# Attention with a threshold: the thresholds of two steps come from one VectorE instruction

## The chip, the cores and the metric

The kernel runs on one core of one Trainium2 chip. The metric is the device time of an execution in microseconds, and the median of the runs stands for a kernel. TensorE is called PE, VectorE DVE, ScalarE ACT, GpSimd POOL and SyncE SP, as the profile does. PE has a separate stream for loading weights, PEld.

## The reference

Three layers follow each other. Only the first is touched here:

```
q, k, v: (4, 8, 576, 64)      tau = 0.02
scores = q @ k^T / sqrt(64)
thresh = max(scores, last axis) - tau
scores = where(scores >= thresh, scores, -1e9)
attn   = exp(scores - max(scores)); attn = attn / (sum(attn) + 1e-9)
x      = attn @ v
```

A rational mixture layer (2304 tokens, 512 to 2048 to 512) and a mixture of eight experts come after it.

## The kernel before

The attention is written as one loop of steps. A step `i` handles 128 query rows, and there are 144 of them: 16 units, each one head of two batches, 1152 rows in nine tiles `t` (0 to 8). Two units share a pair of K and Q tiles, so the pattern of work repeats every eighteen steps. The scores are kept with their sign turned, so the largest score is a minimum.

Every engine runs its own instructions in the order in which the loop emits them. Nothing is reordered, and the framework adds the semaphore waits. An instruction that reads what an earlier instruction of the same engine wrote also waits for that one's semaphore. The loop body of step `i` does this, in this order:

- `emit_s(i + 1)` (L383): PE computes the next step's scores into the PSUM tile `s`. There are three such tiles, so the scores of step `i` need the tile that step `i - 3` has finished with. In every third step this comes after `emit_pv` instead of before it.
- `emit_pv(i - 12)` (L445, L446): PE multiplies the probabilities, transposed, with V. It reads the tile `pt`, twelve steps late.
- `emit_e(i)`: DVE takes the row minimum into `mn[:, 0:1]` (L399, "the reduce"), and ACT takes the exponential into the tile `e`, with that minimum as its bias (L401, "Exp").
- `emit_thr(i)` in some steps, on ACT: `mn[:, 1:2] = mn[:, 0:1] + tau` (L408).
- `emit_p(i - 1)`: DVE compares the scores with the threshold and multiplies by `e` (L415, "the select"). ACT copies that to half precision (L420, "the copy"), and POOL computes what the copy lost (L421, "the remainder"). When `i - 1` is odd, SP then starts a transposing DMA from `php` to `pt` (L424) for that step and the one before it together. `php` is a ring of four such pairs.
- In every third step, `emit_x(..., 0)`: DVE takes the reciprocal of the row sums (L458).
- `emit_thr(i)` in the other steps, on DVE (L410).
- In every third step, `emit_x(..., 1)`: DVE multiplies by the reciprocals (L460).
- Then come steps of a plan written out by hand: PE transposes of Q and K (L242, L247), their copies on ACT (L258 to L269), sums and splits of V (L308, L342, L354, L355), loads, and the DMAs that rotate V.

Which engine makes the threshold is written in a string that repeats every nine steps, `s` for ACT and `v` for DVE:

```
THR = 'svvvsvvvv'
def emit_thr(i):
    mn = st[i][1]
    e = THR[i % len(THR)]
    if e == "s":
        nc.scalar.activation(mn[:, 1:2], mn[:, 0:1], AF.Identity, bias=tauc[:, 1:2])
    else:
        (nc.gpsimd if e == "g" else nc.vector).tensor_scalar(
            mn[:, 1:2], mn[:, 0:1], tauc[:, 1:2], 0.0, op0=ALU.add, op1=ALU.add)
```

So 32 of the 144 thresholds are made by ACT and 112 by DVE. The tile `mn` holds one step's minimum and threshold and has three buffers.

Later in the kernel, the second layer keeps per-column constants in a tile `cvs`. DVE writes two columns of each of its halves at a time (L816 to L821), and ACT reads single columns of it as scales and biases (L939, L940).

Of the kernel before, what the change touches and what calls it, by code (L numbers as in the profile page):

```python
# [9 lines left out]
F32 = mybir.dt.float32  # L10
# [4 lines left out]
AF = mybir.ActivationFunctionType  # L15
ALU = mybir.AluOpType
AX = mybir.AxisListType
PSUM = bass.MemoryType.PSUM
P = 128
# [134 lines left out]
    "xt6": -1,  # L154
}
X_LAG = 0
THR = 'svvvsvvvv'
SUM_ACT = (1, 3)
SUM_AT = (0, 1, 1, 2, 3)
LO_POOL = ()  # L160
# [3 lines left out]
def attention(nc, tc, q, k, v, tau, xT, vs, ident, tail):  # L164
# [7 lines left out]
    def pool(c, name, bufs, **kw):  # L172
        return c.enter_context(tc.tile_pool(name=name, bufs=bufs, side="right", reuse_waits="tile", **kw))

    fix = pool(ctx, "fix", 1)
    sm = pool(ctx, "sm", 3)
# [11 lines left out]
    N = NU * UT  # L188
# [12 lines left out]
    tauc = fix.tile([P, 3], F32, name="tauc")  # L201
# [170 lines left out]
    st = {}  # L372

    def emit_s(i):
        u, t = divmod(i, UT)
        g, hh = divmod(u, 2)
        kt = KT[g].rearrange("p t c -> p (t c)")
        ps = ps_s.tile([P, 2, 512], F32, tag="s", name="s")

        def qk(po, m, qt, bb):  # L380
            for half in range(2):
                c = (2 * bb + half) * 288
                nc.tensor.matmul(  # L383
                    ps[po:po + m, half, 0:288], qz[:, g % 2, hh, t, qt:qt + m],
                    kt[:, c:c + 288], start=True, stop=True)

        if t < 4:
            qk(0, P, 0, 0)
        elif t == 4:
            qk(0, 64, 0, 0)  # L390
            qk(64, 64, 64, 1)
        else:
            qk(0, P, 0, 1)
        st[i] = ps

    def emit_e(i):
        ps = st[i]
        mn = sm.tile([P, 2], F32, tag="mn", name="mn")
        nc.vector.tensor_reduce(mn[:, 0:1], ps[:, :, 0:288], axis=AX.XY, op=ALU.min)  # L399
        e = e_p.tile([P, 2, 288], F32, tag="e", name="e")  # L400
        nc.scalar.activation(e, ps[:, :, 0:288], AF.Exp, bias=mn[:, 0:1], scale=-1.0)  # L401
        st[i] = (ps, mn, e)

    def emit_thr(i):
        mn = st[i][1]
        e = THR[i % len(THR)]
        if e == "s":
            nc.scalar.activation(mn[:, 1:2], mn[:, 0:1], AF.Identity, bias=tauc[:, 1:2])  # L408
        else:
            (nc.gpsimd if e == "g" else nc.vector).tensor_scalar(  # L410
                mn[:, 1:2], mn[:, 0:1], tauc[:, 1:2], 0.0, op0=ALU.add, op1=ALU.add)

    def emit_p(i):
        ps, mn, e = st.pop(i)
        nc.vector.scalar_tensor_tensor(  # L415
            e, ps[:, :, 0:288], mn[:, 1:2], e, op0=ALU.is_le, op1=ALU.mult)
        ring = i // 2 % RING
        ph = php[:, ring, i % 2, 0, :].rearrange("p (a b) -> p a b", a=2)
        pl = php[:, ring, i % 2, 1, :].rearrange("p (a b) -> p a b", a=2)
        nc.scalar.activation(ph, e, AF.Copy)  # L420
        nc.gpsimd.tensor_tensor(pl, e, ph, op=ALU.subtract)  # L421
        if i % 2:
            pt = pt_p.tile([P, 2, UT, P], F16, tag="pt", name="pt")
            nc.sync.dma_start_transpose(  # L424
                out=pt.rearrange("p a b c -> p (a b) c"),
                in_=php[:, ring].rearrange("p a b c -> p (a b c)"))
            st[i - 1] = pt[:, 0]
            st[i] = pt[:, 1]

    def emit_pv(i):  # L430
        u, t = divmod(i, UT)
        g, hh = divmod(u, 2)
        par = g % 2
        pt = st.pop(i)
        parts = ((0, P, 0, 0),) if t < 4 else ((0, 64, 0, 0), (64, 64, 64, 1)) if t == 4 else ((0, P, 0, 1),)
        for po, m, c0, bb in parts:
            if bb == 0:
                seq = [(j, vv, j) for j in range(4) for vv in (vh, vl)]
                seq += [(4, vr, 0), (4, vrl, 0)] + [(4 + j, vr, j) for j in range(1, 5)]
            else:  # L440
                seq = [(j, vv, 5 + j) for j in range(5) for vv in (vr, vrl)]
                seq += [(5 + j, vh, 5 + j) for j in range(4)]
            x = xps[po:po + m, i // 3 % 2, t % 3, :]
            for n, (blk, vv, j) in enumerate(seq):
                nc.tensor.matmul(x, pt[:, blk, c0:c0 + m], vv[:, par, hh, j, :], start=(n == 0), stop=False)  # L445
            nc.tensor.matmul(x[:, D:D1], tiny[:, 0:m], tiny[:, P:P + 1], start=False, stop=True)  # L446
# [5 lines left out]
    def emit_x(u, tg, part):  # L452
        xo = xps[:, (3 * u + tg) % 2]
        if part == 0:
            if tg == 0:
                xfs[u] = x_p.tile([P, UT, D], F32, tag="xf", name="xf")
            rs[0] = sm.tile([P, 3, 1], F32, tag="rinv", name="rinv")
            nc.vector.reciprocal(rs[0], xo[:, :, D:D1])  # L458
        else:
            nc.vector.tensor_tensor(  # L460
                xfs[u][:, 3 * tg:3 * tg + 3], xo[:, :, 0:D], rs[0].to_broadcast([P, 3, D]), op=ALU.mult)
# [41 lines left out]
    def warm(ps, n):  # L503

        for _ in range(n):
            nc.tensor.matmul(ps[:, 0:2 * P], wu[:, 0:P], wu, start=True, stop=True)
# [68 lines left out]
    i = 0  # L575
    emit_s(0)
    while i < N + LAG or plan:
        last = i in pre
        early_pv = last and x_lag(pre[i][0]) == 0
        if i + 1 < N and not early_pv:  # L580
            emit_s(i + 1)
        if 0 <= i - LAG < N:
            emit_pv(i - LAG)
        elif i < LAG:
            warm(xps.rearrange("p a b c -> p (a b c)"), WARM_STEP)
        if i + 1 < N and early_pv:
            emit_s(i + 1)
        if i < N:
            emit_e(i)
        if i < N and THR[i % len(THR)] != "v":  # L590
            emit_thr(i)
        if 0 <= i - 1 < N:
            emit_p(i - 1)
        if last:
            emit_x(*pre[i], 0)
        if i < N and THR[i % len(THR)] == "v":
            emit_thr(i)
        if last:
            emit_x(*pre[i], 1)
        while plan and min(plan) <= i:  # L600
            for f, a in plan.pop(min(plan)):
                f(*a)
        if i == N:
            early.close()
        if i >= N - PRE and tail:
            next(tail)
        i += 1
# [1180 lines left out]
def kernel(ctx, tc, q, k, v, tau, w_in, w_out, a, b, w_gate, w_ogate, w1, w2, out):  # L1788
    nc = tc.nc
    with tc.manual_schedule():  # L1790
        main = ctx.enter_context(tc.tile_pool(name="main", bufs=1))
        dram = ctx.enter_context(tc.tile_pool(name="dram", bufs=1, space=bass.MemoryType.DRAM))
        yd = dram.tile([NT, DM], F32, name="yd")
        part = dram.tile([len(PARTS) * TR * P, DM], F32, name="part")
        ident = main.tile([P, P], F32, name="ident")
        gates = main.tile([P, 4, 2 * E], F32, name="gates")
        L = main.tile([P, NTILE, 2 * E], F32, name="L")
        rt = {
            "gidx": main.tile([P, 2 * NSLOT], I32, name="gidx"),
            "sidx": main.tile([P, 2 * NSLOT], I32, name="sidx"),  # L1800
            "exp": main.tile([P, NSLOT], I32, name="exp"),
            "new": main.tile([P, NSLOT], I32, name="new"),
            "scale": main.tile([P, 2 * NSLOT], F32, name="scale"),
            "nslot": main.tile([P, 1], I32, name="nslot"),
            "more": main.tile([P, 1], I32, name="more"),
        }
        vs = main.tile([P, 2, 2], F32, name="vs")
        nc.scalar.preload_act_table_set("natural_log_exp_and_others")
        R = {}
        mid = ctx.enter_context(tc.tile_pool(name="mid", bufs=1))  # L1810
        xT = mid.tile([P, 4, NTILE, 2, P], F16, name="xT")
        masks.make_identity(nc, ident)
        experts = Experts(ctx, nc, tc, yd, L, rt, R, w1, w2, ident, out, xT)
        gen = moe1(nc, tc, xT, vs, w_in, w_out, a, b, w_gate, w_ogate, gates, ident, yd, part, L,
                   lambda tmp: routing_constants(nc, main, tmp, R), ctx, experts)
        attention(nc, tc, q, k, v, tau, xT, vs, ident, gen)
        for _ in gen:
            pass
        experts.rest()
# [33 lines left out]
```

## Time and profile before

| | |
|---|---|
| median of three runs | 1081.54 us (1081.13 to 1082.86) |
| the profiled execution | 1084.51 us |
| its span, first to last instruction | 1082.7 us |
| mean granted TensorE clock | 0.960 |
| busy: PE, PEld | 962.3 us (89%), 720.7 us (67%) |
| busy: DVE, ACT, POOL | 830.7 us (77%), 718.0 us (66%), 529.3 us (49%) |

The shares are means over the whole span. The attention's 144 steps fill the span from about 10 to 332 us, and the two other layers the rest, so a statement about the thresholds has to be read from the first third. A row of the timeline gives the start in the span, the duration, the engine, the line, the operation and its tiles. In brackets stands the time that the engine was idle before it and what ended that.

### The profile page before, as it was taken

To read this page: it belongs to the slowest core of one execution; us is meant where nothing else is said; L and a number is where in the kernel's file an instruction comes from. 1 tells how busy PE (TensorE), PEld (TensorE's weight loads), DVE (VectorE), ACT (ScalarE), POOL (GpSimd) and SP (SyncE) were. 2 spreads that over 40 slices of the span, in tenths; PEclk is the share of its full clock that TensorE was granted. 3 is DMA by queue.
4 is the path that set the end of the run, shared out by engine and by line. 5 is a ranking of instruction groups with operands and counts; after the bars stand their busy time and mean duration, and the time that the engine had idled before them with its cause. 6 is when DMAs were issued, how large, how long until landed. Compare 5 with 4: busy or idle time off the path is not lost. (4 is left out here: it accounts for less than half of the span.)

```text
span 1082.7 us, 19097 instructions
## 1 busy us (share of the span) xinstructions
PE 962.3 (89%) x7031; PEld 720.7 (67%) x7031; DVE 830.7 (77%) x1364; ACT 718.0 (66%) x1110; POOL 529.3 (49%) x426
## 2 busy tenths in 40 slices
PE   7899859999985788879889999998888799999996
PEld 4677647777755455546556666665557689998995
DVE  4888648888879789998986787898984797665552
ACT  5899759999866677777866656664563455555552
POOL 3588648888774545455464444443532542211111
PEclk8999979999997799999999999999999999999998
DMA  9799999999999422321200221214122111111340
GB/s 206 156 197 217 203 183 200 207 211 220 204 212 234 108 88 88 105 90 59 69 1 30 59 79 47 51 39 127 49 60 78 49 41 49 60 48 40 97 138 22
DMA packets 259525, 119.67 MB, mean 111 GB/s; under 512 B 218080, under 2 KB 246752, under 8 KB 259424
## 3 DMA queue, kind: packets, MB, share of 16 engines
q1 hardware_dynamic: 256160, 108.41, 45.5%
q0 software_dynamic: 3120, 9.96, 2.9%
q8 instruction: 57, 0.93, 0.4%
q14 instruction: 44, 0.36, 0.1%
q10 hardware_dynamic: 144, 0.00, 0.0%
HBM read 82.09 MB, written 13.63 MB: 88 GB/s over the span
## 5 line engine op out<-in xcount | busy, mean ns | idle before, releaser
L915 PE MATMUL h<-xT,wih 128*128 128x384 f16 x768 | 196.0, 339 | 39.3 <-DVE s L932 30.6
L421 POOL TENSOR_TENSOR php<-e,php 128x576 f16<-128x576 f32 x144 | 182.8, 1279 | 91.6 <-ACT php L420 91.3
L383 PE MATMUL s<-kt,qz 128*128 128x288 f32 (+1 forms) x640 | 176.7, 436 | 24.5 <-DVE e L415 14.7
L942 POOL TENSOR_TENSOR t<-t,ah 128x768 f32<-128x768 f32 x48 | 87.7, 1828 | 211.4 <-ACT t L941 195.1
L415 DVE SCALAR_TENSOR_TENSOR e<-s,mn,e 128x576 f32<-128x576 f32 x144 | 116.9, 812 | 36.0 <-ACT e L401 27.4
L915 PEld LDWEIGHTS <-wih 128*128 128x128 f16 x768 | 70.0, 100 | 105.7 <-DVE s L932 40.1
L383 PEld LDWEIGHTS s<-kt,qz 128*128 128x128 f32 (+1 forms) x640 | 99.5, 185 | 55.8 <-issue 22.8
L985 PE MATMUL acc<-woh,gh 128*128 128x512 f32 x288 | 127.0, 441 | 8.4 <-ACT acc L632 3.0
L399 DVE TENSOR_REDUCE mn<-s 128x1 f32<-128x576 f32 x144 | 108.3, 752 | 29.1 <-PE s L383 27.7
L915 PE MATMUL h<-xT,wil 128*128 128x384 f16 x384 | 129.7, 338 | 0.0
L401 ACT ACTIVATE e<-s,mn 128x576 f32<-128x576 f32 x144 | 106.2, 737 | 15.4 <-DVE mn L399 13.9
L985 PE MATMUL acc<-wol,gh 128*128 128x512 f32 x288 | 114.7, 398 | 0.0
L985 PE MATMUL acc<-woh,gl 128*128 128x512 f32 x288 | 114.4, 397 | 0.1
L445 PEld LDWEIGHTS <-pt 128*128 128x128 f16 (+1 forms) x2240 | 90.2, 104 | 32.7 <-issue 14.3
L420 ACT ACTIVATE php<-e 128x576 f16<-128x576 f32 x144 | 97.5, 677 | 17.9 <-DMA pt<-php 17.2
L1681 POOL DMA_INDIRECT out_dram<-os,sidx x19 | 22.6, 1189 | 149.2 <-ACT os L1680 121.0
L967 POOL TENSOR_TENSOR gl<-s,gh 128x768 fp32r<-128x768 f32 x48 | 91.1, 1897 | 7.7 <-issue 4.7
L951 ACT ACTIVATE h<-t,co 128x768 f32<-128x768 f32 x48 | 43.4, 905 | 61.9 <-DVE s L945 19.2
L939 ACT ACTIVATE ah<-h,cvs 128x768 f32<-128x768 f32 x48 | 43.3, 901 | 49.7 <-PE h L915 47.4
L445 PE MATMUL xps<-vr__116,pt 128*128 128x65 f16 (+1 forms) x1280 | 69.2, 198 | 3.4 <-DMA vr__116<-vs__115 2.7
L985 PEld LDWEIGHTS acc<-woh,gh 128*128 128x128 f32 x288 | 55.2, 192 | 25.1 <-ACT part L1002 3.6
L930 DVE SCALAR_TENSOR_TENSOR t<-t,co,h 128x768 f32<-128x768 f32 x48 | 48.4, 1009 | 23.2 <-ACT h L952 13.1
(377 smaller groups left out, 2355.7 us busy)
## 6 DMA issues: line engine op xcount, KB each, us to landing
xT<-in_moe_w_dram SPq DMA_DIRECT2D x80, 512.0 KB
raw<-in_moe_w_in_dram SPq DMA_DIRECT2D x16, 512.0 KB
raw<-in_moe_w_out_dram SPq DMA_DIRECT2D x16, 512.0 KB
vr__116<-vs__115 SPq DMA_DIRECT2D x16, 292.5 KB
yd<-y SPq DMA_DIRECT2D x18, 256.0 KB
raw<-in_k_dram SPq DMA_DIRECT2D x16, 256.0 KB
raw<-in_q_dram SPq DMA_DIRECT2D x16, 256.0 KB
xT<-in_v_dram SPq DMA_DIRECT2D x8, 512.0 KB
```

Source lines behind the costliest of these rows:

```text
L383: nc.tensor.matmul(ps[po:po + m, half, 0:288], qz[:, g % 2, hh, t, qt:qt + m], kt[:, c:c + 288], start=True, stop=True)
L399: nc.vector.tensor_reduce(mn[:, 0:1], ps[:, :, 0:288], axis=AX.XY, op=ALU.min)
L401: nc.scalar.activation(e, ps[:, :, 0:288], AF.Exp, bias=mn[:, 0:1], scale=-1.0)
L415: nc.vector.scalar_tensor_tensor(e, ps[:, :, 0:288], mn[:, 1:2], e, op0=ALU.is_le, op1=ALU.mult)
L420: nc.scalar.activation(ph, e, AF.Copy)
L421: nc.gpsimd.tensor_tensor(pl, e, ph, op=ALU.subtract)
L445: nc.tensor.matmul(x, pt[:, blk, c0:c0 + m], vv[:, par, hh, j, :], start=(n == 0), stop=False)
L915: nc.tensor.matmul(hb[:, 0:n], w[:, k, fc * P:(fc + 1) * P], xT[:, k, t0:t0 + TR, lo, :], start=(i == 0), stop=(i == 11))
L930: lambda: stt(t, t, one, x, op0=ALU.add, op1=ALU.mult),
L942: nc.gpsimd.tensor_tensor(t1, t1, ah, op=ALU.mult)
L967: nc.gpsimd.tensor_tensor(gl, s, gh.bitcast(F32), op=ALU.subtract)
L985: nc.tensor.matmul(acc[r, i], g[:, i * P:(i + 1) * P], w, start=first and m == 0, stop=last and m == 2)
```

## The change

One instruction on DVE makes the thresholds of two steps. The tile `mn` grows to hold two steps' minima and thresholds, still in three buffers. The instruction stands in odd steps, after the step's reduce and before the select of the step before. In even steps there is none. ACT makes no thresholds any more, and nothing else in the loop is moved.

```diff
-THR = 'svvvsvvvv'
...
+    mns = [None]
+
     def emit_e(i):
         ps = st[i]
-        mn = sm.tile([P, 2], F32, tag="mn", name="mn")
+        if i % 2 == 0:
+            mns[0] = sm.tile([P, 2, 2], F32, tag="mn", name="mn")
+        mn = mns[0][:, i % 2]
         nc.vector.tensor_reduce(mn[:, 0:1], ps[:, :, 0:288], axis=AX.XY, op=ALU.min)
...
-    def emit_thr(i):
-        mn = st[i][1]
-        e = THR[i % len(THR)]
-        if e == "s":
-            nc.scalar.activation(mn[:, 1:2], mn[:, 0:1], AF.Identity, bias=tauc[:, 1:2])
-        else:
-            (nc.gpsimd if e == "g" else nc.vector).tensor_scalar(
-                mn[:, 1:2], mn[:, 0:1], tauc[:, 1:2], 0.0, op0=ALU.add, op1=ALU.add)
+    def emit_thr():
+
+        m = mns[0]
+        nc.vector.tensor_scalar(m[:, :, 1], m[:, :, 0], tauc[:, 1:2], 0.0, op0=ALU.add, op1=ALU.add)
...
             emit_e(i)
-        if i < N and THR[i % len(THR)] != "v":
-            emit_thr(i)
+        if i < N and i % 2:
+            emit_thr()
         if 0 <= i - 1 < N:
             emit_p(i - 1)
         if last:
             emit_x(*pre[i], 0)
-        if i < N and THR[i % len(THR)] == "v":
-            emit_thr(i)
         if last:
             emit_x(*pre[i], 1)
```

## Rows read from the trace of the kernel before

**Rows 1.** Busy time by stretch: PE, PEld, DVE, ACT, POOL, then clock, DMA share, GB/s.

```profile
125.00:150.00 25.00, 12.63 (x125) 9.44 (x123) 10.21 (x22) 13.34 (x26) 11.22 (x12) 0.77 1.07 218
225.00:250.00 25.00, 24.58 (x270) 18.25 (x270) 20.97 (x42) 23.39 (x45) 20.50 (x19) 1.00 1.14 198
```

**Rows 2.** Instructions on the tile `mn` (ns min/median/max), and waits they ended.

```profile
L415 DVE SCALAR_TENSOR_TENSOR e<-s,mn,e x144: 796/809/819, 15.4 to 330.6; 128x576 f32<-128x576 f32 x144
L410 DVE TENSOR_SCALAR mn<-mn,tauc x112: 183/204/208, 16.1 to 330.2; 128x1 f32<-128x1 f32 x112
L408 ACT ACTIVATE mn<-mn,tauc x32: 282/284/307, 14.2 to 323.7; 128x1 f32<-128x1 f32 x32
...
  ACT mn L408: 7.5, 9
```

**Rows 3.** Timeline of DVE, steps 81 to 83, and eighteen steps later.

```profile
201.79 0.76 DVE L399 TENSOR_REDUCE mn<-s 128x1 f32<-128x576 f32 x1 [0.60 <-PE s L383]
202.47 0.81 DVE L415 SCALAR_TENSOR_TENSOR e<-s,mn,e 128x576 f32<-128x576 f32 x1
203.19 0.75 DVE L399 TENSOR_REDUCE mn<-s 128x1 f32<-128x576 f32 x1
203.85 0.81 DVE L415 SCALAR_TENSOR_TENSOR e<-s,mn,e 128x576 f32<-128x576 f32 x1
204.58 0.20 DVE L410 TENSOR_SCALAR mn<-mn,tauc 128x1 f32<-128x1 f32 x1
204.70 0.75 DVE L399 TENSOR_REDUCE mn<-s 128x1 f32<-128x576 f32 x1
...
237.63 0.76 DVE L399 TENSOR_REDUCE mn<-s 128x1 f32<-128x576 f32 x1 [0.59 <-PE s L383]
```

**Rows 4.** Timeline of DVE: small instructions, each reading what the one before wrote.

```profile
155.03 0.16 DVE L654 TENSOR_SCALAR t<-tp 128x1 f32<-128x1 f32 x1 [0.20 <-PE tp L332]
155.22 0.15 DVE L662 TENSOR_SCALAR g<-t 128x1 int32<-128x1 int32 x1
```

**Rows 5.** The line L821: strided small instructions with a scalar read from a tile.

```profile
L821 DVE TENSOR_SCALAR cvs<-cvs,co x16: 214/224/226, 344.8 to 546.7; 128x4 f32<-128x4 f32 x16
```

**Rows 6.** Timeline of DVE, step 83, a step with reciprocals.

```profile
206.65 0.17 DVE L458 RECIPROCAL rinv<-xps 128x3 f32<-128x3 f32 x1
206.74 0.18 DVE L410 TENSOR_SCALAR mn<-mn,tauc 128x1 f32<-128x1 f32 x1
206.85 0.36 DVE L460 TENSOR_TENSOR xf<-xps,rinv 128x192 f32<-128x192 f32 x1
```

**Rows 7.** Timeline of ACT, step 81.

```profile
202.64 0.74 ACT L401 ACTIVATE e<-s,mn 128x576 f32<-128x576 f32 x1 [0.45 <-DVE mn L399]
203.28 0.28 ACT L408 ACTIVATE mn<-mn,tauc 128x1 f32<-128x1 f32 x1
203.47 0.67 ACT L420 ACTIVATE php<-e 128x576 f16<-128x576 f32 x1
```

**Rows 8.** Timeline of PE: first score matrices of steps 83, 89 and 95.

```profile
203.42 0.97 PE L383 MATMUL s<-kt,qz 128*128 128x288 f32 x3 [0.16 <-DVE e L415]
...
215.41 0.48 PE L383 MATMUL s<-kt,qz 128*128 128x288 f32 x1 [0.50 <-DVE mn L410]
...
227.10 0.41 PE L383 MATMUL s<-kt,qz 128*128 128x288 f32 x1
```

**Rows 9.** Timeline of DVE, step 93.

```profile
225.28 0.76 DVE L399 TENSOR_REDUCE mn<-s 128x1 f32<-128x576 f32 x1 [0.38 <-PE s L383]
225.95 0.81 DVE L415 SCALAR_TENSOR_TENSOR e<-s,mn,e 128x576 f32<-128x576 f32 x1
```

**Rows 10.** Waits from 250 to 332 us: waiter, releaser, total us, times, longest.

```profile
ACT php L420 <- DMA pt<-php: 13.7, 9, 3.7
```

**Rows 11.** Timeline of ACT and DVE in the second layer.

```profile
477.62 0.90 ACT L939 ACTIVATE ah<-h,cvs 128x768 f32<-128x768 f32 x1
...
479.42 0.16 DVE L816 TENSOR_TENSOR cvs<-sc,vs 128x4 f32<-128x4 f32 x1
```

## The prediction

> **What bounds the kernel now.** I read the busy times by stretch first, then the timeline of one repeated group of eighteen steps on each engine, then the waits. In an undisturbed stretch of the attention four engines are close together [rows 1]: PE 24.58 of 25 us, ACT 23.39, DVE 20.97, and the DMA engines are full (share 1.14) at full clock. PE idles 0.42 us there (2%), so it is the pacemaker, with ACT next; DVE idles 4.03 us (16%). The group is a strict pattern: the reduce of step 81 starts at 201.79 us and that of step 99 at 237.63 us [rows 3], so eighteen steps take 35.84 us. On the timeline the pattern stands undisturbed in steps 27 to 44 and 63 to 119. In between, an ACT sum waits for V, and PE is busy only 12.63 of 25 us [rows 1]. After 284 us ACT's copies wait 13.7 us, nine times, for transposing DMAs to free `php` [rows 10]; there the DMAs set the pace.
>
> What can change is thus local: an instruction that PE or ACT waits for comes earlier or later by tenths of a microsecond, and the reader has to ask at each place whether that wait was the last to end.
>
> **What is removed.** ACT loses 32 thresholds of 0.28 us. The copy behind one starts 0.19 us after it [rows 7], since neighbours overlap, so each gives 0.19 us: 6.1 us in all, four of them (0.76 us) in a group of eighteen. DVE loses 112 of about 0.20 us [rows 2]. Their price is again the pitch: threshold at 204.58, next reduce at 204.70, so 0.12 us [rows 3]. In every third step even that is nothing: reciprocal 206.65, threshold 206.74, multiply 206.85 [rows 6]. The multiply needs the reciprocal, which ends at 206.82, so without the threshold it would start at about 206.85 as well. In a group, 14 thresholds are on DVE, 6 of them between reciprocal and multiply; 8 x 0.12 = 0.96 us goes.
>
> **What is added.** 72 thresholds of 2 x 128 elements on DVE, strided. No row has this form. Below it lies the 0.16 us of a small instruction [rows 4], above it the 0.224 us of a strided one with four elements and a scalar from a tile [rows 5]. I take 0.20 us, that of the old one, which has the same operands [rows 2].
>
> The place costs more than the instruction. Today the select follows the reduce of the next step 0.68 us after its start (201.79 to 202.47), before the reduce's 0.76 us are over [rows 3], because it doesn't read what that reduce writes. In odd steps the new threshold does, and the select reads the threshold. An instruction that reads its predecessor's result starts about 0.03 us after its end (155.03 + 0.16 = 155.19, start 155.22) [rows 4]. So the select starts at 0.76 + 0.03 + 0.20 + 0.03 = 1.02 us after the reduce in place of 0.68: 0.34 us later (0.30 to 0.37 with the bounds). Nine odd steps add 3.06 us to DVE in a group. Less 0.96, DVE's chain grows by 2.1 us in 35.84. Its 16% idle time is 5.8 us a group, so DVE can hold that; the question is who waits.
>
> A sentence of the Trainium skill speaks the other way. Its page "VectorE: DVE Perf Modes", section "The DRAIN you can't avoid", says that the flush after a DVE instruction comes whether or not a semaphore follows, and that a semaphore costs nothing extra. By that rule only the count matters: 40 fewer instructions of 0.20 us, 8 us off DVE. The rows disagree: the independent select starts 0.08 us before the reduce's end [rows 3], the dependent instruction 0.03 us after [rows 4].
>
> **Who waits for the late select.** Behind it on DVE stand the next reduce, the reciprocal and the multiply. Outside, PE waits for it to give the score tile back (two steps' scores later), and ACT's copy of its result. The remainder on POOL and the transposing DMA hang on the odd-numbered select, which stands in an even step and has its threshold early. No DMA is moved, and nothing on SP's or POOL's queue passes anything.
>
> First unit of the group, t = 0 to 8: the scores of step 83 start at 203.42, waiting for the select of step 80 [rows 8], which starts at 202.47 [rows 3]. It comes 0.34 us later, and so does PE. ACT's copy in that step waited for the ACT threshold until 203.47 [rows 7]; now it waits for the select until 202.47 + 0.34 + 0.81 + 0.04 = 203.66. So ACT is 0.19 us late in spite of the removed threshold, until the next removed one, at t = 4, gives 0.19 back. PE has room for its own delay at t = 8: the scores of step 89 wait 0.50 us [rows 8], for a select that waits for ACT's Exp, which is on time again. Net: 0.
>
> Second unit: the scores of step 95 start at 227.10 with no wait [rows 8]. They need the select of step 92, which starts at 225.95 behind the reduce of 225.28 [rows 9]. With the pair's threshold it starts at 225.28 + 0.76 + 0.03 + 0.20 + 0.03 = 226.30 and ends at 227.11; a score matrix starts 0.14 us after such an end (202.47 + 0.81 = 203.28 to 203.42) [rows 3, 8], at 227.25. That is 0.15 us late, and nothing up to the next group gives it back. Net: +0.15 us.
>
> Four second units lie in the undisturbed stretches (steps 36 to 44, 72 to 80, 90 to 98, 108 to 116): 4 x 0.15 = +0.6 us. Elsewhere I count nothing, and name the cover: before step 14 and around 125 to 150 us the waits for V; after 284 us the waits for the transposing DMAs [rows 1, 10]. Where that cover is gone, an odd step can cost its 0.34 us, and a removed ACT threshold that is the last wait gives up to 0.28 us; ACT's threshold ended nine waits of DVE, 7.5 us [rows 2], but most of each was Exp before it. What is late at the end of the attention is late at the end of the span, one for one.
>
> **Sum.** The profiled execution took 1084.51 us, its span 1082.7, so 1.8 us lie around it; I expect 1085.1 and a span of 1083.3. The median of the runs is 3.0 us below the profiled one: 1081.54 + 0.6 = 1082.1 us. A change of this kernel under 0.2% (2.2 us) I call the same.
>
> **Rivals.**
>
> - *ACT's relief is the path* (faster). ACT is busy 23.39 of 25 us [rows 1] and 6.1 us leave it. If every removed threshold shortens the path and no select holds a copy back, the time is 1081.5 - 6.1 = 1075.4; I expect half of it at most, about 1078.5. Against it: in the step followed above the late select takes the 0.19 us back. Chance 0.20.
> - *The late selects become the path* (slower). If in the undisturbed stretches (18 + 57 = 75 steps, 37 of them odd) PE waits for each late select, 37 x 0.34 = 12.6 us come in and at most 75/18 x 0.96 = 4.0 us go out: 1090.1. It decides where a select has less than 0.34 us to spare before PE needs its tile; I found two such places in one group, and one is absorbed. With one more per unit exposed it is about 1085. Chance 0.25.
> - *The wait that is false* (slower). The pair's threshold writes around the minimum that Exp of the same step reads. Were ranges compared as a whole, the threshold would wait for Exp's end: in step 81 until 202.64 + 0.74 = 203.38 [rows 7] in place of 202.55, 0.83 us more, over 72 pairs 60 us: 1141 or more. Against it: ACT's L939 at 477.62 reads a `cvs` column that lies between the columns that L816 writes at 479.42 [rows 11]; it is emitted after that L816 and ran before it all the same. So a strided write doesn't hold such a reader. Chance 0.03.
> - *Only the count matters* (faster). An instruction that reads its neighbour's result pays nothing extra. Then DVE loses 40 x 0.20 = 8 us and ACT 6.1; if half of ACT's is path, 1078.5, and with DVE's 1075. The row of the dependent pair [rows 4] is against it. The skill's section named above is this rule. Chance 0.02.
>
> **Numbers.** The likeliest, absorbed delays, has 0.50; its own range is 1080.2 to 1083.6 us. The range of 1078 to 1087 takes in half of ACT's relief below and, above, about half of the late selects. Faster by over 0.2%: 0.20 + 0.02 = 0.22. Slower: 0.25 + 0.03 = 0.28. The same: 0.50.
>
> **What the profile after would show.** L408 is gone, and L410's successor counts 72 at about 0.2 us. In odd steps the select starts about 1.02 us after its reduce, in even ones 0.68. The group that held steps 81 to 98 takes about 36.0 us. Waits of PE for the select grow, waits of DVE for ACT's threshold vanish. The prediction is wrong if the group gets shorter than 35.6 us or longer than 36.3, if the threshold of a pair waits for ACT, or if the late stretch, from 284 us on, doesn't swallow shifts but turns them into another order of DMAs.

## The result, and the profile after

| | before | after |
|---|---|---|
| median of the runs | 1081.54 us | 1092.76 us (1088.62 to 1094.2) |
| ratio, 95% interval | | 1.0090 (1.0064 to 1.0116) |
| profiled execution, its span | 1084.51, 1082.7 us | 1089.07, 1087.3 us |
| busy DVE, ACT, POOL | 830.7, 718.0, 529.3 us | 862.9, 717.2, 530.2 us |

The changed kernel is 0.9% slower, 9.7 us by the ratio. I forecast 1082.1 us and a range up to 1087: wrong. DVE has 40 fewer instructions and is busy 32 us longer.

First the busy times by stretch, as in [rows 1] (PE, PEld, DVE, ACT, POOL, clock, DMA share, GB/s):

```profile
125.00:150.00 25.00, 15.56 (x157) 11.84 (x154) 13.74 (x26) 15.06 (x28) 12.61 (x13) 0.80 1.03 222
225.00:250.00 25.00, 23.01 (x259) 17.17 (x256) 22.51 (x38) 21.50 (x41) 18.82 (x18) 1.00 1.08 202
```

In the undisturbed stretch DVE went from 20.97 to 22.51 us of 25 and PE from 24.58 to 23.01: PE now waits, and DVE works longer on fewer instructions (38 for 42). The view of the tile `mn`, as in [rows 2], tells which instruction it is, and below the dots who waits for the tile's instructions (us, times):

```profile
L402 DVE TENSOR_REDUCE mn<-s x144: 734/749/759, 11.2 to 333.9; 128x1 f32<-128x576 f32 x144
L414 DVE SCALAR_TENSOR_TENSOR e<-s,mn,e x144: 806/817/820, 13.3 to 337.3; 128x576 f32<-128x576 f32 x144
L410 DVE TENSOR_SCALAR mn<-mn,tauc x72: 228/422/1300, 12.9 to 334.7; 128x2 f32<-128x2 f32 x72
...
  PE s L382: 32.4, 41
  ACT php L419: 26.1, 33
```

In the same view of the kernel before, these two were:

```profile
  PE s L383: 20.8, 27
  ACT php L420: 0.7, 1
```

The reduce and the select are as before. The pair's threshold (L410) has 228 ns at least, 422 at the median and 1300 at most, where the old one had 183, 204 and 208 [rows 2]. A spread from 228 to 1300 with one shape and one place in the order says that it waits for something while it counts as busy. The timeline of DVE and POOL in two odd steps shows for what:

```profile
206.30 0.76 DVE L402 TENSOR_REDUCE mn<-s 128x1 f32<-128x576 f32 x1
207.09 0.23 DVE L410 TENSOR_SCALAR mn<-mn,tauc 128x2 f32<-128x2 f32 x1
207.43 0.82 DVE L414 SCALAR_TENSOR_TENSOR e<-s,mn,e 128x576 f32<-128x576 f32 x1
...
209.98 2.51 POOL L420 TENSOR_TENSOR php<-e,php 128x576 f16<-128x576 f32 x2 [0.68 <-ACT php L419]
210.46 0.76 DVE L402 TENSOR_REDUCE mn<-s 128x1 f32<-128x576 f32 x1 [0.18 <-PE s L382]
211.25 1.26 DVE L410 TENSOR_SCALAR mn<-mn,tauc 128x2 f32<-128x2 f32 x1
212.62 0.82 DVE L414 SCALAR_TENSOR_TENSOR e<-s,mn,e 128x576 f32<-128x576 f32 x1
```

At 207.09 POOL is idle: 0.23 us, and the select starts 1.13 us after its reduce. At 211.25 POOL has just begun its second remainder (the row counts two back to back, ending at 209.98 + 2.51 = 212.49): the threshold ends at 211.25 + 1.26 = 212.51, 0.02 us behind it, and the select starts 2.16 us after its reduce. Set against POOL's instructions in the whole trace, 46 of the 72 begin while POOL runs and end 0.02 to 0.07 us after its instruction; they take 0.735 us on the mean. Two of these meet only the end of POOL's instruction and take 0.228 us, so 44 wait. The 26 others take 0.228 to 0.231 us. So 46 x (0.735 - 0.228) = 23.3 us of DVE are waiting.

The group of eighteen steps, from the reduce of step 81 to that of step 99, takes 37.99 us for the 35.84 of [rows 3]:

```profile
202.36 0.76 DVE L402 TENSOR_REDUCE mn<-s 128x1 f32<-128x576 f32 x1 [0.59 <-PE s L382]
...
240.35 0.76 DVE L402 TENSOR_REDUCE mn<-s 128x1 f32<-128x576 f32 x1 [0.60 <-PE s L382]
```

### The profile page after: what moved, and what is told of

It is laid out like the page before. It is cut to its first block, busy times and chain, and to the rows that moved or that the text cites. A ratio compares the mean times of both kernels' runs of the same rounds, so it can differ in the third digit from the quotient of the medians.

```text
span 1087.3 us, 18957 instructions
## 1 busy us (share of the span) xinstructions
PE 958.3 (88%) x7031; PEld 718.7 (66%) x7031; DVE 862.9 (79%) x1324; ACT 717.2 (66%) x1078; POOL 530.2 (49%) x426
## 5 line engine op out<-in xcount | busy, mean ns | idle before, releaser
L382 PE MATMUL s<-kt,qz 128*128 128x288 f32 (+1 forms) x640 | 173.2, 429 | 35.9 <-DVE e L414 32.4
L912 PEld LDWEIGHTS <-wih 128*128 128x128 f16 x768 | 69.9, 100 | 105.3 <-DVE s L929 39.7
L419 ACT ACTIVATE php<-e 128x576 f16<-128x576 f32 x144 | 97.7, 679 | 31.6 <-DVE e L414 22.8
```

Of the source, the lines that this page charges most:

```text
L382: nc.tensor.matmul(ps[po:po + m, half, 0:288], qz[:, g % 2, hh, t, qt:qt + m], kt[:, c:c + 288], start=True, stop=True)
L912: nc.tensor.matmul(hb[:, 0:n], w[:, k, fc * P:(fc + 1) * P], xT[:, k, t0:t0 + TR, lo, :], start=(i == 0), stop=(i == 11))
```

## The experiments

Theory P: the two-element form waits until POOL's running instruction ends, and that makes the loss. Rival L: the late select makes it (the place behind the reduce), whoever runs beside it. Each experiment shows its edit, against the changed kernel or the one before; the ratios are to the kernel before.

**Two one-element instructions in the pair's place** (place alone).

```diff
-        nc.vector.tensor_scalar(m[:, :, 1], m[:, :, 0], tauc[:, 1:2], 0.0, op0=ALU.add, op1=ALU.add)
+        for k in (1, 0):
+            nc.vector.tensor_scalar(
+                m[:, k, 1:2], m[:, k, 0:1], tauc[:, 1:2], 0.0, op0=ALU.add, op1=ALU.add)
```

> The changed kernel, but the pair's two thresholds are two one-element instructions at the pair's place, so the select of odd steps still depends on the reduce in front of it. Theory P (the two-element form waits until GpSimd's running instruction ends, and that makes the loss): every threshold takes 0.15 to 0.22 us whatever POOL does, the select of an odd step starts about 1.2 us after its reduce everywhere, and a group of eighteen steps takes 35.9 to 36.5 us; time 1081 to 1086 us. Rival L (the late select alone makes the loss, whoever runs beside it): the place is the same and the select even 0.1 us later, so a group takes 38.0 us or more; time 1089 to 1096 us.

1081.81 us, ratio 1.0016 (1.0000 to 1.0033). The thresholds' row in the view of the tile `mn`:

```profile
L411 DVE TENSOR_SCALAR mn<-mn,tauc x144: 202/210/215, 12.8 to 329.4; 128x1 f32<-128x1 f32 x144
```

and the timeline of an odd step beside a running POOL:

```profile
205.53 2.52 POOL L422 TENSOR_TENSOR php<-e,php 128x576 f16<-128x576 f32 x2 [0.68 <-ACT php L421]
206.01 0.76 DVE L402 TENSOR_REDUCE mn<-s 128x1 f32<-128x576 f32 x1 [0.17 <-PE s L382]
206.81 0.33 DVE L411 TENSOR_SCALAR mn<-mn,tauc 128x1 f32<-128x1 f32 x2
207.25 0.82 DVE L416 SCALAR_TENSOR_TENSOR e<-s,mn,e 128x576 f32<-128x576 f32 x1
```

POOL runs from 205.53 to 208.05 and the two thresholds take 0.33 us together all the same. The select comes 1.24 us after its reduce, later than the changed kernel's undisturbed ones, and the group takes 36.62 us (198.42 to 235.04), a little over the 36.5 expected. P holds: without the waits the loss is 0 to 3.6 us, not 9.7. In that, ACT's relief hides a part of what the place costs. Against ACT's relief alone (below), which has the same 144 instructions in the old places, the place costs 1.12 us a group (36.62 for 35.50) and 0.25% of the whole (1.0016 for 0.9991), 2.7 us.

**The two-element form in the old places** (waits alone): the kernel before, with DVE's 112 thresholds made on a tile of their own with a second element that nobody reads.

```diff
+    mnr = fix.tile([P, 3, 2, 2], F32, name="mnr")
...
-        mn = sm.tile([P, 2], F32, tag="mn", name="mn")
+        mn = mnr[:, i % 3, 0]
...
-            (nc.gpsimd if e == "g" else nc.vector).tensor_scalar(
-                mn[:, 1:2], mn[:, 0:1], tauc[:, 1:2], 0.0, op0=ALU.add, op1=ALU.add)
+            m = mnr[:, i % 3]
+            nc.vector.tensor_scalar(m[:, :, 1], m[:, :, 0], tauc[:, 1:2], 0.0, op0=ALU.add, op1=ALU.add)
```

> The kernel before, with its order and its split between DVE and ACT; only the 112 thresholds on DVE are made with a second element that nobody reads (a tile of its own, set to zero once). Theory P: the 112 take 0.23 us where POOL is idle and up to 1.3 us where it runs, 0.4 to 0.6 us on the mean, each ending 0.02 us after POOL's instruction; that is 3 to 5 us of DVE in a group, whose idle time there is 5.8 us, so a group grows by 1 to 4 us and the time is 1086 to 1110 us. Rival L: no select depends on a later reduce, so nothing changes: thresholds at 0.2 us, group 35.8 us, time 1079.4 to 1083.7 us.

1101.80 us, ratio 1.0172. Two more runs (below) came out about as slow though nothing in them waited for POOL, against both theories, and all three had a new tile that moved others. With the new tile filled up to 512 bytes:

> The run with the unread second element again, with the new tile filled up to 512 bytes, so that php, pt and the others stand as in the kernel before, less 512 bytes. The waits for POOL stay (112 thresholds, 78 us in all against 22 us), all in the order of the kernel before. Theory P: a group of eighteen takes about 38 us as in the first try, the time is 1085 to 1094 us (the loss of the first try less that of the tiles' place). Rival L: 1079 to 1084 us, all of the first try's loss was the place of the tiles.

1092.24 us, ratio 1.0085 (1.0054 to 1.0116). The thresholds' row in the view of their tile, and below it two rows of the timeline:

```profile
L416 DVE TENSOR_SCALAR mnr<-mnr,tauc x112: 199/743/1221, 14.8 to 334.7; 128x2 f32<-128x2 f32 x112
```

```profile
206.82 1.28 POOL L426 TENSOR_TENSOR php<-e,php 128x576 f16<-128x576 f32 x1 [1.03 <-ACT php L425]
...
207.21 0.92 DVE L416 TENSOR_SCALAR mnr<-mnr,tauc 128x2 f32<-128x2 f32 x1
```

The threshold ends at 208.13, POOL's remainder at 208.10. No select depends on the next reduce here and the loss is there, 9.2 us; the group takes 38.03 us (202.08 to 240.11). Rival L alone is out. The waiting is longer than in the changed kernel, though, about 54 us (76.0 in place of 22.0 for the 112), and the loss is no larger: only a part of the waiting reaches the end.

**The same pair in a form with an accumulator.**

```diff
-            m[:, :, 1], m[:, :, 0], tauc[:, 1:2], 0.0, op0=ALU.add, op1=ALU.add)
+            m[:, :, 1], m[:, :, 0], tauc[:, 1:2], 0.0, op0=ALU.add, op1=ALU.add, accum_out=acc)
```

> The changed kernel, with the same two-element threshold in the same place, reading and writing the same addresses; it also writes out its accumulator to a column that nobody reads. If the hold by POOL belongs to every two-element instruction with this operand pattern, the 46 long ones stay (up to 1.3 us) and the time is 1090 us or more. If it belongs to a mode that the instruction runs in and the form with an accumulator doesn't have that mode, all 72 take 0.2 to 0.25 us and the read of the accumulator 0.08 us behind each, the group of eighteen is 36.4 to 37.0 us as with two one-element instructions, and the time is 1081 to 1085 us. The Trainium skill, page "SBUF — State Buffer", section "Who interferes with whom", says the second: it takes the form that also writes out its accumulator from the list of those that grab the pair of ports shared with GpSimd.

1102.26 us, ratio 1.0198, although no threshold waited for POOL: 0.215 us each, group 36.29 us. That fitted neither theory. Where the tiles stand was the difference, and with `acc` filled up to 512 bytes it went:

> The two-element threshold with an accumulator again, its tile filled up to 512 bytes, so that the others keep their place. Thresholds took 0.215 us there with POOL running or not, and the group 36.3 us. If the place of the tiles was the rest, the time is 1080 to 1085 us, that of two one-element instructions. If the accumulator's read costs more than its 0.08 us by another way, it stays at 1095 us or more.

1082.92 us, ratio 1.0006 (0.9981 to 1.0031), group 36.31 us (200.01 to 236.32). The thresholds' row in the view of the tile `mn`, then the timeline of an odd step:

```profile
L411 DVE TENSOR_SCALAR_CACHE_REDUCE mn<-mn,tauc x72: 213/215/217, 14.3 to 329.6; 128x2 f32<-128x2 f32 x72
```

```profile
207.02 2.52 POOL L422 TENSOR_TENSOR php<-e,php 128x576 f16<-128x576 f32 x2 [0.69 <-ACT php L421]
207.50 0.76 DVE L403 TENSOR_REDUCE mn<-s 128x1 f32<-128x576 f32 x1 [0.18 <-PE s L383]
208.30 0.21 DVE L411 TENSOR_SCALAR_CACHE_REDUCE mn<-mn,tauc 128x2 f32<-128x2 f32 x1
208.44 0.08 DVE L411 DVE_READ_ACCUMULATOR mn<-mn,tauc 128x1 f32 x1
208.62 0.82 DVE L416 SCALAR_TENSOR_TENSOR e<-s,mn,e 128x576 f32<-128x576 f32 x1
```

The same two elements of the same tile, the same place, POOL running from 207.02 to 209.54, and no wait. So it is not the operands that make the wait but the plain form, TENSOR_SCALAR in the trace, where this one is TENSOR_SCALAR_CACHE_REDUCE. The Trainium skill, page "SBUF — State Buffer", section "Who interferes with whom", states a rule for it: copy, cast and the plain tensor_scalar can enter a mode with two ports that shares a pair with GpSimd, the second to issue is blocked for the other's whole instruction, and the accumulator form and the reduce are exempt. For the threshold and the reduce these runs agree: 0.735 us against 0.228, long ones that end 0.02 us or a little more behind POOL's instruction, 0.215 us with the accumulator, and reduces of 0.76 us beside a running POOL. That ports are what the instruction waits for is the page's account; no run shows them.

**POOL's remainder left out**, in both kernels (the low half of the weights stays zero, so the outputs lack it).

```diff
+    nc.gpsimd.memset(php.rearrange('p a b c d -> p (a b c d)'), 0.0)
...
-        nc.gpsimd.tensor_tensor(pl, e, ph, op=ALU.subtract)
```

> The changed kernel without POOL's remainder in each step (the low half of the weights stays zero, set once). POOL's remainders held 28 of the 46 long thresholds, for 19.0 of 23.3 us of waiting; the other 18 were held by the low half of V, for 4.3 us. Theory P: only those behind the low half of V stay long, some 0.1 to 0.5 us each, the sum of the thresholds falls from 39.7 us to 18 to 23 us, and the kernel is level with the kernel before without the remainder within 4 us (the pair was 9 to 11 us slower with it). Rival L: the distance to the kernel before without the remainder stays 9 to 11 us.

> The kernel before without POOL's remainder (the low half of the weights stays zero, set once): the base for the run without the remainder of the changed kernel. Transposing DMAs no longer wait for POOL, which took 1.28 us in each step behind the copy; if they set the pace the time falls by a few us, otherwise it stays: 1072 to 1083 us. Both theories expect the same here.

1081.62 (1.0002; 0.9988 to 1.0017) and 1077.45 us (0.9977; 0.9958 to 0.9995). By these ratios the pair's distance fell from 9.7 us to 0.25%, 2.7 us (the two medians are 4.2 us apart). The row of the thresholds in the changed kernel without remainders:

```profile
L412 DVE TENSOR_SCALAR mn<-mn,tauc x72: 228/228/831, 16.1 to 324.9; 128x2 f32<-128x2 f32 x72
```

The median is the undisturbed 228 ns; they add up to 20.2 us in place of 39.7. Eight still wait, 3.8 us in all, for POOL's instructions that make the low half of V. With the remainders away most of the loss is away; what is left, 2.7 us, lies within the 0 to 3.6 us of the kernel with two one-element instructions.

**ACT's relief alone**: the kernel before with `THR = 'vvvvvvvvv'`.

> The kernel before, with the 32 thresholds of ACT moved to DVE as one-element instructions, in the place that DVE's have: the relief of ACT alone. If ACT's relief is worth what the prediction's rival said (half of 6.1 us), the time is about 1078.5 us. If ACT has slack there, as the prediction's first theory has it, DVE's 32 more (0.12 us each, 3.8 us in all) lie in its idle time and the time is 1080 to 1083 us. Theories P and L don't differ here.

1080.36 us, ratio 0.9991 (0.9973 to 1.0008): 1.0 us, with the rival's 3 us just outside the interval. In the whole there is no gain clear of noise. But ACT isn't without effect in the undisturbed stretch: the group takes 35.50 us for 35.84.

```profile
198.93 0.76 DVE L399 TENSOR_REDUCE mn<-s 128x1 f32<-128x576 f32 x1 [0.59 <-PE s L383]
...
234.43 0.76 DVE L399 TENSOR_REDUCE mn<-s 128x1 f32<-128x576 f32 x1 [0.60 <-PE s L383]
```

Of the 0.76 us that ACT loses in a group, 0.34 shortens it, nearly the half that the rival had. Over the 75 undisturbed steps that is 1.4 us.

**No threshold at all**: the edit is against the changed kernel.

```diff
-        nc.vector.tensor_reduce(mn[:, 0:1], ps[:, :, 0:288], axis=AX.XY, op=ALU.min)
+        nc.vector.tensor_tensor_reduce(
+            jnk, ps[:, :, 0:288], tauc[:, 1:2].unsqueeze(2).to_broadcast([P, 2, 288]), scale=1.0, scalar=1e30,
+            op0=ALU.add, op1=ALU.min, accum_out=mn[:, 0:1])
...
-            e, ps[:, :, 0:288], mn[:, 1:2], e, op0=ALU.is_le, op1=ALU.mult)
+            e, ps[:, :, 0:288], mn[:, 0:1], e, op0=ALU.is_le, op1=ALU.mult)
...
-        if i < N and i % 2:
-            emit_thr()
```

> No threshold instruction at all: the reduce adds tau to each score and takes the minimum of that, and Exp takes this value as its bias (each row's weights are larger by one factor, which the division by their sum takes out). The instruction writes its sums to a tile that nobody reads. No select depends on the reduce in front of it and no two-element instruction is left. If the reduce still takes about 0.75 us (bounds 0.7 and 0.95), theory P and rival L both give a time below the kernel before: DVE loses 112 x 0.12 = 13 us, ACT 6.1 us, in all 1070 to 1080 us. If the reduce takes over 0.9 us, DVE gains more than it loses and Exp comes later: 1085 us or more.

1098.96 us, ratio 1.0148, again with a new tile that moves others. With it filled up to 1536 bytes:

> The reduce that adds tau itself, with no threshold at all, its tile filled up to 1536 bytes, so that the others keep their place. The reduce took 0.757 us and the read of its accumulator 0.083 us, where the reduce before took 0.748 us and its thresholds 0.12 us of DVE each. If the place of the tiles made the loss of the first try, the time is 1070 to 1080 us; if the form has a cost of its own, 1085 us or more.

1080.50 us, ratio 0.9985 (0.9962 to 1.0008). A miss, between the two ranges: no threshold is left, none waits, and the time is the same within the measurement. DVE didn't lose 13 us, though: 144 reads of the accumulator came in (0.083 us each), and its busy time fell from 830.7 to 824.6 us. The group takes 35.52 us (195.74 to 231.26), as with ACT's relief alone (35.50), where DVE makes all 144 thresholds and is busy 831.8 us. So one-element thresholds on DVE in the old places cost the group nothing that shows.

**The select on the exponential**, in the kernel before, with no threshold either, but with two inputs in SBUF.

```diff
-            e, ps[:, :, 0:288], mn[:, 1:2], e, op0=ALU.is_le, op1=ALU.mult)
+            e, e, etau, e, op0=ALU.is_ge, op1=ALU.mult)
```

> The kernel before without any threshold: the select compares the exponential with exp(-tau), one number for all rows, instead of the score with the row's threshold (scores on the very edge may fall on the other side). The score tile comes free after Exp, 0.8 us earlier, and DVE loses 112 x 0.12 = 13 us. Against it: the select now has both inputs in SBUF. If that makes it wait for POOL's running remainder as the two-element threshold did (mean wait 0.5 us in each step), DVE's chain is as long as in the run with the unread second element and the time 1090 to 1110 us. If it doesn't wait, the time is 1068 to 1080 us.

1098.64 us, ratio 1.0148, all tiles in their old place. Its tile `e` shows both sides pay:

```profile
L416 DVE SCALAR_TENSOR_TENSOR e<-e,tauc x144: 797/1161/1929, 15.0 to 343.5; 128x576 f32<-128x576 f32 x144
...
L422 POOL TENSOR_TENSOR php<-e,php x144: 1266/1788/1934, 16.7 to 346.0; 128x576 f16<-128x576 f32 x144
```

The select went from 0.81 to 1.16 us at the median and POOL's remainder from 1.28 to 1.79. So taking the thresholds away in this way costs more than they do.

**The place of the tiles.** 32 unused bytes a partition, in the kernel before; then `php` alone moved, the others alone, and other places at multiples of 256.

```diff
+    pad = fix.tile([P, 8], F32, name="pad")
+    nc.gpsimd.memset(pad, 0.0)
```

> The kernel before with one unused tile of 32 bytes a partition in front of others, which moves most tiles of the attention by 32 bytes (php, from which the transposing DMAs read, from a multiple of 256 bytes to 32 below one); no instruction of the loop is changed. The three runs with a new tile (the unread second element, the accumulator, the reduce with tau) have moved php off a multiple of 256 bytes, the other runs have not. In those three SP's issue of a transposing DMA takes 3.3 us on the mean, 238 to 239 us in all 72, against 201 to 216 us in the others, and they are 16 to 21 us slower than the kernel before. If the place of the tiles does that, this run too has about 239 us and takes 1095 to 1104 us. If it was the added instructions, it takes 1079 to 1084 us.

> The kernel before with unused tiles that put php alone 32 bytes below a multiple of 256 (the tiles under it move by 512 bytes, the ones above it stay). The run with everything 32 bytes lower took 23 us more. If the place of php, from which the transposing DMAs read, makes that, this run takes 1097 to 1107 us and the issues of the 72 transposing DMAs 235 to 243 us; if the place of the tiles that they write (pt) or of the loads makes it, 1078 to 1085 us and 205 to 218 us.

> The kernel before with php and the tiles above it in their place, and pt, the exponentials, the loads of Q and K and the rest under it 32 bytes lower. The counterpart of the run with php alone: 1078 to 1085 us if php makes the 23 us, 1097 to 1107 us if one of these does.

> The kernel before with one unused tile of 192 bytes, so that pt, the exponentials, Q and K as loaded and their transposed tiles also start at multiples of 256 bytes; php and the values stay. If a start at a multiple of 256 bytes also helps what the DMAs write, the time falls to 1070 to 1078 us; if only the place of php counts, it stays at 1079 to 1084 us.

> As the run before, and the rotated values (vr, written by DMAs) start at a multiple of 256 bytes too, php and vs at multiples of 512. If the rotating DMAs gain, the time is 2 to 6 us under that of the run before; if not, within 2 us of it.

| moved | us | ratio, 95% interval |
|---|---|---|
| all by 32 bytes | 1105.01 | 1.0199 (1.0157 to 1.0240) |
| `php` alone by 32 | 1102.07 | 1.0199 (1.0166 to 1.0231) |
| the others by 32 | 1080.71 | 1.0005 (0.9979 to 1.0032) |
| `pt` and more to multiples of 256 | 1085.77 | 1.0057 (1.0039 to 1.0076) |
| and the rotated values | 1080.87 | 1.0001 (0.9986 to 1.0017) |

The first run came out 1 us above its range, the one with `pt` and more at multiples of 256 between its two. The rows of the line that issues the transposing DMAs, first of the kernel before, then with `php` moved:

```profile
L424 SPq DMA_TRANSPOSE pt<-php x72: 1742/2688/5412, 21.7 to 338.0; - x72
...
  ACT php L420: 17.2, 12
```

```profile
L428 SPq DMA_TRANSPOSE pt<-php x72: 2432/3230/4924, 19.1 to 354.4; - x72
...
  ACT php L424: 29.0, 17
```

The issue of one took 3.23 us at the median for 2.69, and ACT's copies waited 29.0 us for them, not 17.2. `php`, which these DMAs read, makes the 2%; `pt`, which they write, doesn't. The median issue separates the runs: 3.23 to 3.28 us in the five that moved `php` off a multiple of 256 bytes, 2.53 to 2.74 in all others. The changed kernel is one of the others:

```profile
L423 SPq DMA_TRANSPOSE pt<-php x72: 1744/2576/6168, 18.9 to 342.5; - x72
```

So none of this is in its loss. Why multiples of 256 for `pt` and more cost 0.6% without the rotated values and nothing with them, I can't say.

## Why the prediction was wrong

**The step that failed** is the price of what is added: "No row has this form. Below it lies the 0.16 us of a small instruction [rows 4], above it the 0.224 us of a strided one with four elements and a scalar from a tile [rows 5]. I take 0.20 us". The duration without a wait was about right, 0.228 us. The upper bound was wrong: 44 of 72 waited for POOL, and the mean of all is 0.55 us. From 0.20 that is 25 us of DVE, none of it in the sum, the range or a rival. The row behind the upper bound couldn't show it: 15 of the 16 instructions of L821 began while POOL was idle, and one met only the end of a POOL instruction. POOL stands in the prediction only as one that waits for the select; that DVE could wait for POOL with no dependency between them was not considered.

And the trace of before had the row. In the second layer's preparation a tensor_scalar of two elements runs beside a remainder on POOL; the timeline of before shows it next to its like:

```profile
342.93 0.16 DVE L662 TENSOR_SCALAR g<-t 128x2 int32<-128x2 int32 x1
342.95 1.27 POOL L472 TENSOR_TENSOR xn<-xf,xn 128x576 f16<-128x576 f32 x1 [9.44 <-ACT xn L471]
...
343.00 1.25 DVE L666 TENSOR_SCALAR g<-t 128x2 int32<-128x2 int32 x1
```

L662 started 0.02 us before POOL and took 0.16 us; L666 started 0.05 us after POOL and took 1.25, ending at 344.25, behind POOL's 344.22. I had taken my bounds from the nearest operand pattern; the nearest operation with more than one element beside a running POOL would have given 0.16 to 1.25 us. With it the sum can be made: POOL is busy 20.50 of 25 us there [rows 1], so most thresholds would meet it (46 of 72 did).

**The place** was priced too low as well, but by too little to leave the range. An odd select was to start 1.02 us after its reduce; undisturbed it starts at 1.13, because the start behind the threshold takes 0.10 to 0.11 us (207.09 + 0.23 = 207.32 to 207.43), not 0.03. That select takes its threshold as a scalar; the row that I used [rows 4] is of another instruction. Accumulator form and two one-element ones lengthen the group by 0.47 and 0.78 us where I had 0.15, and so beyond the 36.3 us that I had named as a sign of being wrong, with no wait for POOL in it. The whole grows by 0.06% and 0.16%: within "the same", as forecast, in part because ACT's relief gives some of it back.

**The rivals.** "The late selects become the path" names the right place and nearly the right time, 1090.1, but that is luck, for its reason isn't there: 0.34 us more alone didn't do it. (Of its 75 steps 38 are odd, not 37, which makes it 1090.4.) With the waits, the nine odd selects of steps 81 to 98 start 0.76 + 0.03 + 0.54 + 0.10 = 1.43 us after their reduces on the mean, 0.75 later than the 0.68 of before, and then PE does wait: 32.4 us for the select, 41 times, where it was 20.8 us, 27 times, for the select or the threshold behind it; and ACT's copies, which had waited once for the select, wait 22.8 us for it, 32 times (the 26.1 us of the view take in one wait for a threshold). "ACT's relief is the path" fails in the whole (1.0 us, within noise) but had nearly the right share in the undisturbed group (0.34 of 0.76 us). "Only the count matters" falls with two kernels of the same 144 one-element thresholds on DVE: behind the reduce they take 1.12 us a group more than in the old places. "The wait that is false" falls with the undisturbed thresholds: at 207.09 the Exp of the step before is still running (206.63 to 207.37); it reads a minimum of the same pair, and the threshold doesn't wait for it. The late stretch swallowed some of the delay, as hoped: from 250 to 332 us the copies waited 4.4 us for transposing DMAs where they had waited 13.7 [rows 10].

Of 23.3 us of waiting for POOL about 8 us reach the end, an estimate: 9.7 less the 1.7 of the two one-element instructions, which is the place's 2.7 less the 1.0 of ACT's relief. How much each covering wait took of the rest was not separated.

## What to carry to other kernels

Merging two small DVE instructions can put them into another class: at two elements, read from and written to SBUF, the plain tensor_scalar waited for whatever GpSimd was running and took up to 1.30 us, and at one element, or with an accumulator, it didn't wait. Nor did a two-element one whose source is a PSUM tile, as the trace of before shows in the second layer:

```profile
453.65 1.84 POOL L967 TENSOR_TENSOR gl<-s,gh 128x768 fp32r<-128x768 f32 x1
454.13 0.16 DVE L654 TENSOR_SCALAR t<-h 128x2 f32<-128x2 f32 x1 [1.21 <-PE h L799]
```

Six of eight of these began beside a running POOL, and all eight took 0.15 to 0.16 us; no experiment changed the source alone. Before pricing a merged instruction, look in the trace for the same operation with more than one element beside a busy POOL, and read its maximum, not its median. And when an experiment adds a tile, keep the others where they stand: here 32 bytes cost more than the change under study.

No version with the same outputs was measurably faster than the kernel before; those that came near (ACT's relief alone, the reduce with tau) have 1 in their interval.

## What the runs showed that I had not expected

The start of `php` decides 2% of the whole: 32 bytes below a multiple of 256 the transposing DMAs that read it were issued in 3.23 us in place of 2.69, and the kernel took 21 us more. The Trainium skill, page "DMA: Bandwidth & Descriptors", section "How a descriptor splits into AXI transactions", says that a read which starts off a multiple of 256 bytes begins at the boundary below and pays for the unused bytes; the runs agree as far as that goes, since the read tile counts and the written one doesn't, but no run shows the transactions.

A select with both inputs in SBUF and POOL's remainder slowed each other, 0.81 to 1.16 and 1.28 to 1.79 us at the median: unlike the two-element threshold, which let POOL finish at its own speed.
